# A list schedule that knows TensorE's clock gate

## The chip, the cores and the metric

The kernel runs on one core of a Trainium2 chip. The metric is the device time of one execution in microseconds (us). A core has five engines that run side by side, each through its own queue in order: TensorE (PE, matrix products into PSUM), VectorE (DVE), ScalarE (ACT), GpSimd (POOL) and SyncE (SP, which issues transfers here).

## What is computed

A residual vector quantizer between two depthwise convolutions, on two sequences of 16000 steps with 512 channels in bfloat16:

```python
B, T, D, K = 2, 16000, 512, 3
Nq, C = 4, 8
...
for i in range(K):
    z = z + xp[:, i:i+T, :] * dw_enc[i][None, None, :]
z = _silu(z)
res = z
q = jnp.zeros_like(z)
for s in range(Nq):
    cb = codebooks[s]
    d2 = |res|^2 - 2 res.cb + |cb|^2          # (shortened)
    idx = d2.argmin(-1)
    sel = cb[idx]
    q = q + sel
    res = res - sel
...
for i in range(K):
    y = y + qp[:, i:i+T, :] * dw_dec[i][None, None, :]
```

Each of four stages picks the nearest of eight codewords for each time step and subtracts it from the residual.

## The kernel before

The sequence is cut into 18 tiles (0 to 17): 6 and 8 blocks of 128 steps, fourteen tiles of 16 blocks, then 8 and 6. A tile passes through these kinds of steps, by the names that the scheduler uses:

- "load" and "pad": transposing transfers, and two small copies on GpSimd
- "taps", "exp", "plus1", "recip", "gate": the first convolution and the activation, in two halves (h = 0, 1) of the channels. Taps are multiplications by a scalar and sums on VectorE; exp and recip are table functions on ScalarE, each in its own table; plus1 adds 1 to the exponential and gate multiplies
- "score0", "decide", "win0": small products of the residual with the codebooks, the choice of stages 0 to 2 on VectorE in a long chain of small steps (with transposes and corrections on TensorE), and the one-hot matrix of the choices, which is copied out of PSUM into OHW
- "resid": 24 products that subtract the chosen codewords, each followed by an evacuation
- "score3", "decide3", "win3": the last stage
- "back": the products that give the output, their copies out of PSUM on ScalarE, and the stores

All steps are first collected with their dependences, then put in order by a list scheduler in Python while the program is built, and issued in that order. Nothing of it runs on the chip; it fixes the order of each engine's queue, and which engine takes a step that two engines can do. It works with a cost in microseconds for each step, and among the steps that can start earliest takes the one with the lowest rank:

```python
    def rank(self, s):
        w = self.when[s["k"][0]][self.part(s)]
        return w[0] + s["k"][1] + w[1] * s["k"][2]
...
            full = [d for d in ("ACT", "DVE") if held[d] >= self.quota[d]]
            ...
                dest = "DVE" if load("DVE", t) + self.share[self.part(s)] < load("ACT", t) else "ACT"
...
            if isinstance(s["e"], tuple) and e == "ACT" and t + s["c"]["ACT"] > max(at[s["n"]], clock["DVE"]) + s["c"]["DVE"] + self.slack[self.part(s)]:
                return inf, None
```

SHARE weighs the two engines where a residual product is to be emptied, SLACK where a small step may go to either, and WHEN holds two numbers for each kind of step and each part of the program (tiles 0 to 2, the middle, tiles 15 to 17). A product costs the time of a full clock:

```python
    def mm(n):
        return max(0.06, 0.004 + n / 2380)
```

The residual is the step on which most of the choice bears. With ScalarE as the taker, an identity product first brings the old residual into PSUM and the evacuation is a copy; with VectorE it is an addition (cut):

```python
                    def mms(s=s, u=u, i=i, zg=zg, box=box):
                        on_act = box["dest"] == "ACT"
                        for k0 in range(0, GH, 4):
                            nk = min(4, GH - k0)
                            o = ps(box)[:, k0 * P:(k0 + nk) * P]
                            if on_act:
                                nc.tensor.matmul(o, lhsT=IDENT, rhs=zg[:, k0:k0 + nk, :], start=True, stop=False)
                            nc.tensor.matmul(o, lhsT=CBN[s, u][:, i * P:(i + 1) * P], rhs=W[:, k0:k0 + nk, PADC:PADC + P],
                                             start=not on_act, stop=True)

                    def evac(zg=zg, box=box):
                        v = ps(box)[:, 0:GH * P].rearrange("p (k c) -> p k c", c=P)
                        if box["dest"] == "ACT":
                            nc.scalar.copy(zg, v)
                        else:
                            nc.vector.tensor_tensor(out=zg, in0=zg, in1=v, op=ALU.add)
                    j = add("PE", {"ACT": 2 * mm(GH * P), "DVE": mm(GH * P)}, key, mms, [tok, ("OHW", n % NOH, 0), ("CBN", s, u), "I"], [],
                            take=("A", box), dest="ANY", mm={"ACT": 2 * ((GH + 3) // 4), "DVE": (GH + 3) // 4})
                    add(None, {"ACT": act_psum(GH * P), "DVE": dve(GH * P)}, key, evac, [], [tok], free=box, after=[j])
```

The taps, where either engine may multiply, and the activation:

```python
                dst, src, w = (tb if k else ta)[:, c], X[:, i, k:k + G, :].rearrange("p g c -> p (g c)"), WENC[:, k, i:i + 1]
                either({"ACT": act(R), "DVE": dve(R, 3.84) + 0.06}, key, lambda dst=dst, src=src, w=w: nc.scalar.mul(dst, src, w),
                       lambda dst=dst, src=src, w=w: nc.vector.tensor_scalar(out=dst, in0=src, scalar1=w, scalar2=None, op0=ALU.mult),
                       allx + ["WENC"], [("TB" if k else "TA", c)])
            if k == 1:
                tt(ta, ta, tb, ALU.add, dve(2 * R, 1.92), key, [("TB", 0), ("TB", 1)], [("TA", 0), ("TA", 1)])
        tt(Z, v(ta), v(tb), ALU.add, dve(2 * R, 1.92), key, [(t, c) for t in ("TA", "TB") for c in range(2)], zt)
        add("ACT", act(2 * R), ("exp", n, h), lambda: nc.scalar.activation(v(ex), Z, ACT.Exp, scale=-1.0), zt, [("EX", sl), "ACTTAB"], hold="E")
        either({"ACT": act(2 * R), "DVE": dve(2 * R, 3.84)}, ("plus1", n, h), lambda: nc.scalar.add(ex, ex, 1.0),
               lambda: nc.vector.tensor_scalar(out=ex, in0=ex, scalar1=1.0, scalar2=None, op0=ALU.add), [], [("EX", sl)])
```

PSUM is used as four pairs of banks ("A" takes a pair, "S" one bank):

```python
    PS = [psum.tile([P, 1024], F32, name=f"ps{b}") for b in range(NA)]
```

Of the kernel before, what the change touches and what calls it, by code (L numbers as in the profile page):

```python
# [16 lines left out]
class Plan:  # L17
# [5 lines left out]
    LATENCY = {"PE": 0.2, "ACT": 0.22, "DVE": 0.15, "POOL": 0.25, "SP": 0.1}  # L23
    TABLE = 1.28
    CHUNK, FIRST, FETCH = 128, 33, 4.2

    def __init__(self, pairs, edges, share, slack, quota, when):
        self.steps, self.writer, self.readers = [], {}, {}
        self.pairs, self.edges, self.share, self.slack, self.quota, self.when = pairs, edges, share, slack, quota, when
# [22 lines left out]
    def rank(self, s):  # L52
        w = self.when[s["k"][0]][self.part(s)]
        return w[0] + s["k"][1] + w[1] * s["k"][2]

    def order(self):
        steps = self.steps
        inf = float("inf")
        left = [len(s["deps"]) for s in steps]
        rank = [self.rank(s) for s in steps]  # L60
        users = [[] for _ in steps]
        for s in steps:
            for d in s["deps"]:
                users[d].append(s["n"])
        at = [0.0] * len(steps)
        clock = {e: 0.0 for e in self.LATENCY}
        waiting = {e: [] for e in clock}
        held = {e: 0 for e in clock}
        banks = [0.0] * (2 * self.pairs)
        table = None  # L70
        run, fetched = self.FIRST, 0.0
        self.busy = {e: 0.0 for e in clock}
        out = []

        def cost(s, e):
            return s["c"][e] if isinstance(s["c"], dict) else s["c"]

        def place(kind, t):
            if kind == "A":
                return min((max(banks[j], banks[j + 1], t), 0, j) for j in range(0, 2 * self.pairs, 2))  # L80
            return min((max(banks[j], t), -max(banks[j ^ 1], t), j) for j in range(2 * self.pairs))

        def load(d, t):
            return max(clock[d] - t, 0.0) + held[d] + sum(cost(steps[m], d) for m in waiting[d]
                                                        if at[m] <= t + 1.0 and (d == "DVE" or not isinstance(steps[m]["e"], tuple)))

        def many(s, dest):
            return s["mm"][dest] if isinstance(s["mm"], dict) else s["mm"]

        def late(m, t, c):  # L90

            return max(0.0, fetched - (t + c * (self.CHUNK - run) / m)) if run + m > self.CHUNK else 0.0

        def look(s, e):

            t = max(at[s["n"]], clock[e])
            if s["take"]:
                dest = s["dest"]
                if dest == "ANY":
                    full = [d for d in ("ACT", "DVE") if held[d] >= self.quota[d]]  # L100
                    if len(full) == 2:
                        return inf, None
                    if full:
                        dest = "ACT" if full[0] == "DVE" else "DVE"
                    else:
                        dest = "DVE" if load("DVE", t) + self.share[self.part(s)] < load("ACT", t) else "ACT"
                elif dest and held[dest] >= self.quota[dest]:
                    return inf, None
                kind = s["take"][0]
                t = place(kind[dest] if isinstance(kind, dict) else kind, t)[0]  # L110
                return t + late(many(s, dest), t, cost(s, dest) if s["dest"] == "ANY" else s["c"]), dest
            if isinstance(s["e"], tuple) and e == "ACT" and t + s["c"]["ACT"] > max(at[s["n"]], clock["DVE"]) + s["c"]["DVE"] + self.slack[self.part(s)]:
                return inf, None
            if s["mm"]:
                t += late(s["mm"], t, s["c"])
            return t, None

        def open_(n):
            e = steps[n]["e"]
            for e in e if isinstance(e, tuple) else (e,) if e else ():  # L120
                waiting[e].append(n)

        for s in steps:
            if not left[s["n"]]:
                open_(s["n"])
        while len(out) < len(steps):
            (t, dest), _, n, e = min(((look(steps[n], e), rank[n], n, e) for e, names in waiting.items() for n in names),
                                     key=lambda q: (q[0][0], q[1], q[2], q[3]))
            assert t < inf
            s = steps[n]  # L130
            for w in waiting.values():
                if n in w:
                    w.remove(n)
            c = cost(s, dest if s["take"] and s["dest"] == "ANY" else e)
            if s["take"]:
                kind, box = s["take"]
                kind = kind[dest] if isinstance(kind, dict) else kind
                j = place(kind, t)[2]
                box["banks"] = [j, j + 1] if kind == "A" else [j]
                for j in box["banks"]:  # L140
                    banks[j] = inf
                box["dest"] = dest
                if s["dest"] == "ANY":
                    steps[n + 1]["e"] = dest
                if dest:
                    held[dest] += 1
            elif s["box"] is not None:
                s["box"]["dest"] = e
            if s["hold"] and table != s["hold"]:
                table = s["hold"]  # L150
                c += self.TABLE
            if s["mm"]:
                m = many(s, dest)
                run += m
                if run > self.CHUNK:
                    run -= self.CHUNK
                    fetched = t + c * (m - run) / m + self.FETCH
            s["t"], s["d"], s["on"] = t, c, e
            clock[e] = t + c
            self.busy[e] += c  # L160
            end = t + c + s["tail"]
            if s["free"]:
                if s["free"]["dest"]:
                    held[s["free"]["dest"]] -= 1
                for j in s["free"]["banks"]:
                    banks[j] = end + self.LATENCY[e]
            out.append(s)
            for u in users[n]:
                ue = steps[u]["e"]
                at[u] = max(at[u], t + c + self.AGAIN[e] if ue == e else end + self.LATENCY[e])  # L170
                left[u] -= 1
                if not left[u]:
                    open_(u)
        self.span = max(clock.values())
        return out
# [3 lines left out]
def kernel(  # L179
# [27 lines left out]
    PAIR = 1  # L207
    NX, NE, NZ, NOH, NY = 2, 3, 4, 4, 4
    NA = 4
    SHARE = (14.79, 1.9, -1.12)  # L210
    SLACK = (0.29, -1.21, -1.81)
    QUOTA = {"ACT": 3, "DVE": 4}
    WHEN = {"setup": ((0.456, 0.998), (1.178, 0.655), (0.941, 0.735)), "load": ((-1.978, 0.878), (-1.958, 0.738), (-1.958, 0.878)),
            "pad": ((-1.401, 0.11), (-1.77, 0.139), (-2.325, 0.134)), "taps": ((-0.056, 0.558), (-0.338, 0.569), (0.293, 1.087)),
            "exp": ((1.265, 0.168), (1.206, 0.297), (1.399, 0.12)), "plus1": ((1.063, 0.361), (0.294, 0.173), (0.161, 0.493)),
            "recip": ((0.527, 0.735), (0.419, 0.023), (1.274, 0.525)), "gate": ((-0.093, 0.61), (0.842, 0.495), (1.223, 0.636)),
            "score0": ((-0.15, 0), (1.321, 0.2), (0.126, 0)), "decide": ((1.789, 0.412), (0.54, 0.196), (0.843, 0.939)),
            "win0": ((2.222, 0), (2.206, 0), (3.035, 0.025)), "resid": ((1.585, 0.81), (1.683, 0.7), (1.984, 0.791)),
            "score3": ((2.128, 0.749), (2.581, 0.231), (3.178, 1.482)),
            "decide3": ((1.618, 0.493), (2.772, 0.723), (3.423, 0.605)), "win3": ((2.988, 0.158), (3.009, 1.183), (3.689, 0.224)),  # L220
            "back": ((2.837, 0.37), (3.155, 1.136), (4.316, 0.509))}
    assert B == len(SIZES) and T >= GM * P and GM <= 16

    xf = x.flatten_outer_dims()
# [65 lines left out]

    plan = Plan(NA, (3, len(tiles) - 3), SHARE, SLACK, QUOTA, WHEN)
    add = plan.add
# [506 lines left out]
```

## Time and profile before

| | |
|---|---|
| time, median of 3 | 740.62 us (738.44 to 742.37) |
| profiled execution | 735.13 us, span 733.4 us |
| busy: VectorE, ScalarE, TensorE, GpSimd | 676.7, 665.8, 528.2, 140.0 us |
| mean granted TensorE clock | 0.927 of full |

"Busy" is the time in which an engine has an instruction under way. A row of the costliest groups gives line, engine, operation, what is written and read, the count, then busy time and mean ns of one, then the idle time of the engine just before these instructions and the instruction that ended most of it. The answer on waits gives for each pair of waiter and releaser the sum in us, the number and the longest. The granted clock is a record of its own: it is 1.00 or 0.50 at any time here.

```profile
PEclk9997875897999999998999999999997999999998
```

Each digit is one fortieth of the span, in tenths of the full clock.

### The profile page before, as it was taken

To read this page: it belongs to the slowest core of one execution; us is meant where nothing else is said; L and a number is where in the kernel's file an instruction comes from. 1 tells how busy PE (TensorE), PEld (TensorE's weight loads), DVE (VectorE), ACT (ScalarE), POOL (GpSimd) and SP (SyncE) were. 2 spreads that over 40 slices of the span, in tenths; PEclk is the share of its full clock that TensorE was granted. 3 is DMA by queue.
4 is the path that set the end of the run, shared out by engine and by line. 5 is a ranking of instruction groups with operands and counts; after the bars stand their busy time and mean duration, and the time that the engine had idled before them with its cause. 6 is when DMAs were issued, how large, how long until landed. Compare 5 with 4: busy or idle time off the path is not lost.

```text
span 733.4 us, 23788 instructions
## 1 busy us (share of the span) xinstructions
PE 528.2 (72%) x10374; PEld 269.3 (37%) x10441; DVE 676.7 (92%) x1249; ACT 665.8 (91%) x592; POOL 140.0 (19%) x199
## 2 busy tenths in 40 slices
PE   1055733787868779886797778777867888898994
PEld 0032221443333344443343333433434444444442
DVE  8979999999999999998989999999988999998992
ACT  7868999998999999999899999998987999999755
POOL 2111013030112114332011212212112040111204
PEclk9997875897999999998999999999997999999998
DMA  5554536523361825438073562809343050113306
GB/s 113 95 98 81 129 54 139 91 60 67 109 109 30 146 81 116 110 62 172 11 163 69 87 111 74 156 25 185 59 76 94 10 130 24 61 59 116 117 11 200
DMA packets 148047, 67.78 MB, mean 92 GB/s; under 512 B 139776, under 2 KB 139808, under 8 KB 147944
## 3 DMA queue, kind: packets, MB, share of 16 engines
q1 hardware_dynamic: 137088, 33.06, 26.9%
q0 software_dynamic: 10640, 32.78, 14.8%
q8 instruction: 81, 1.33, 0.8%
q10 hardware_dynamic: 216, 0.43, 0.2%
q14 instruction: 22, 0.18, 0.1%
HBM read 0.43 MB, written 32.77 MB: 45 GB/s over the span
## 4 chain that ended last, share of the span: by engine, by line
DVE 32%; PE 22%; issue 6%; ACT 6%; SPq 1%; DMA 0%; POOL 0%; POOLq 0%; DVEq 0%; ACTq 0%
DVE ZB L668 9%; PE ps L660 7%; PE ps L526 5%; PE ps L659 5%; DVE ZB L333 5%; DVE TB L491 3%; ACT ZB L666 2%; DVE TA L333 2%; ACT YB L725 2%; PE ps L717 2%; DVE OHW L637 2%; DVE TA L491 2%; DVE EX L498 1%; DVE KEY L333 1%; PE ps L631 1%
## 5 line engine op out<-in xcount | busy, mean ns | idle before, releaser
L666 ACT CAST ZB<-ps 128x1024 bf16<-128x1024 f32 (+2 forms) x301 | 259.5, 959 | 34.3 <-PE ps L660 30.9
L660 PE MATMUL ps<-OHW,CBN 128*128 128x512 bf16 (+1 forms) x768 | 271.6, 390 | 17.8 <-DVE ZB L668 7.4
L659 PE MATMUL ps<-ZB,IDENT 128*128 128x512 bf16 (+1 forms) x540 | 212.5, 394 | 28.5 <-ACT ZB L666 10.0
L748 POOL DMA_DIRECT2D out_dram<-YB x130 | 77.6, 601 | 344.8 <-ACT YB L725 341.4
L668 DVE TENSOR_TENSOR ZB<-ZB,ps 128x1024 bf16<-128x1024 bf16 (+2 forms) x131 | 136.7, 1056 | 6.2 <-PE ps L660 5.2
L725 ACT CAST YB<-ps 128x1024 bf16<-128x1024 f32 x126 | 124.7, 1044 | 5.8 <-PE ps L526 2.5
L660 PEld LDWEIGHTS <-CBN 128*128 128x128 bf16 x768 | 75.7, 100 | 140.2 <-issue 70.7
L526 PE MATMUL ps<-ZB 128*32 128x64 bf16 x8064 | 93.1, 202 | 40.2 <-DVE ZB L333 22.4
L496 ACT ACTIVATE EX<-ZB 128x4096 bf16<-128x4096 bf16 (+2 forms) x36 | 115.7, 3215 | 5.1 <-DVE ZB L333 4.9
L508 ACT ACTIVATE EX<-EX 128x4096 bf16<-128x4096 bf16 (+2 forms) x36 | 114.8, 3199 | 0.5 <-DVE EX L498 0.3
L526 PEld LDWEIGHTS <-ZB 128*32 128x32 bf16 x8064 | 80.0, 99 | 88.9 <-issue 66.3
L491 DVE TENSOR_SCALAR TB<-XT,WENC 128x2048 bf16<-128x2048 bf16 (+2 forms) x139 | 93.0, 686 | 0.2
L717 PE MATMUL ps<-WDEC,OHW 128*128 128x512 bf16 x215 | 70.7, 400 | 17.4 <-DVE ZB L668 5.3
L659 PEld LDWEIGHTS <-IDENT 128*128 128x128 bf16 x540 | 54.2, 100 | 67.5 <-issue 13.8
L333 DVE TENSOR_TENSOR ZB<-ZB,EX 128x4096 bf16<-128x4096 bf16 (+2 forms) x36 | 73.5, 2042 | 1.3 <-ACT EX L508 1.1
L333 DVE TENSOR_TENSOR ZB<-TA,TB 128x4096 bf16<-128x4096 bf16 (+2 forms) x36 | 73.4, 2039 | 0.6 <-ACT TB L490 0.4
L333 DVE TENSOR_TENSOR TA<-TA,TB 128x4096 bf16<-128x4096 bf16 (+2 forms) x36 | 73.0, 2027 | 0.4
L469 POOL COPY XT<-XT 128x508 bf16<-128x508 bf16 x18 | 35.5, 1972 | 69.5 <-DVE TB L491 65.5
L491 DVE TENSOR_SCALAR TA<-XT,WENC 128x2048 bf16<-128x2048 bf16 (+2 forms) x70 | 47.7, 692 | 0.6 <-DMA XT<-in_x_dram 0.2
L468 POOL COPY XT<-XT 128x508 bf16<-128x508 bf16 x18 | 24.3, 1353 | 125.1 <-DMA XT<-in_x_dram 125.1
L631 PE MATMUL ps<-IDENT,OHA 128*32 128x128 bf16 x504 | 24.2, 235 | 30.1 <-DVE OHA L333 12.9
L717 PEld LDWEIGHTS <-OHW 128*128 128x128 bf16 x252 | 23.6, 101 | 48.8 <-issue 22.5
(99 smaller groups left out, 433.2 us busy)
## 6 DMA issues: line engine op xcount, KB each, us to landing
out_dram<-YB POOLq DMA_DIRECT2D x33, 448.0 KB, 3.8
out_dram<-YB POOLq DMA_DIRECT2D x28, 512.0 KB, 4.5
XT<-in_x_dram SPq DMA_TRANSPOSE x252, 3.2
out_dram<-YB POOLq DMA_DIRECT2D x30, 60.0 KB, 3.9
out_dram<-YB POOLq DMA_DIRECT2D x31, 2.0 KB, 2.2
out_dram<-YB POOLq DMA_DIRECT2D x2, 224.0 KB, 2.6
YB<-in_dw_dec_dram ACTq DMA_DIRECT2D x1, 384.0 KB, 4.2
out_dram<-YB POOLq DMA_DIRECT2D x1, 384.0 KB
```

The source lines that it names most:

```text
L333: add("DVE", cost, key, lambda: nc.vector.tensor_tensor(out=out, in0=a, in1=b, op=op), reads, writes, **kw)
L491: lambda dst=dst, src=src, w=w: nc.vector.tensor_scalar(out=dst, in0=src, scalar1=w, scalar2=None, op0=ALU.mult),
L496: add("ACT", act(2 * R), ("exp", n, h), lambda: nc.scalar.activation(v(ex), Z, ACT.Exp, scale=-1.0), zt, [("EX", sl), "ACTTAB"], hold="E")
L508: nc.scalar.add_instruction(mybir.InstActivation(name=nc.get_next_instruction_name(), engine=mybir.EngineType.Activation, func=ACT.Reciprocal,
L526: nc.tensor.matmul(o[HB * q:HB * (q + 1), u * ZW:(u + 1) * ZW].rearrange("p (s c) -> p s c", s=2), lhsT=blk, rhs=both, start=False, stop=( ...
L659: nc.tensor.matmul(o, lhsT=IDENT, rhs=zg[:, k0:k0 + nk, :], start=True, stop=False)
L660: nc.tensor.matmul(o, lhsT=CBN[s, u][:, i * P:(i + 1) * P], rhs=W[:, k0:k0 + nk, PADC:PADC + P], start=not on_act, stop=True)
L666: nc.scalar.copy(zg, v)
L668: nc.vector.tensor_tensor(out=zg, in0=zg, in1=v, op=ALU.add)
L717: nc.tensor.matmul(o, lhsT=W[:, k, PADC:PADC + P], rhs=WDEC[u], start=True, stop=not wrap)
L725: add("ACT", act_psum(1024), key, lambda k=k, box=box, Y=Y, k0=k0: nc.scalar.copy(Y[:, 2 * (k - k0):2 * (k - k0) + 2, :].rearrange("p g d ...
L748: nc.gpsimd.dma_start(out=view[p0:p1, lo:hi, :], in_=Y[p0:p1, lo - g0:hi - g0, :])
```

## The change

The scheduler's cost of a product becomes dependent on TensorE's recent use. It counts the work of TensorE in windows of 3.413 us. Where a window held less than half of its length in work, the next one runs at half clock, in which the products of a step take longer by a factor that depends on the kind: 2.0 for the residual and the output, 1.5 for the one-hot windows, 1.4 for the scores, 1.5 for others. The first number of a pair in GATE is the share of the step's time that counts as work. No products are added to keep TensorE busy. The constants SHARE, SLACK and WHEN are new as well. The purpose is an order that suits the times which products really take.

```diff
--- before.py
+++ after.py
@@ -23,6 +23,8 @@
     LATENCY = {"PE": 0.2, "ACT": 0.22, "DVE": 0.15, "POOL": 0.25, "SP": 0.1}
     TABLE = 1.28
     CHUNK, FIRST, FETCH = 128, 33, 4.2
+    SPAN, BUSY = 3.413, 0.5
+    GATE = {"resid": (1.0, 2.0), "back": (1.0, 2.0), "win0": (0.6, 1.5), "win3": (0.6, 1.5), "score0": (0.25, 1.4), "score3": (0.25, 1.4)}
 
     def __init__(self, pairs, edges, share, slack, quota, when):
         self.steps, self.writer, self.readers = [], {}, {}
@@ -53,6 +55,22 @@
         w = self.when[s["k"][0]][self.part(s)]
         return w[0] + s["k"][1] + w[1] * s["k"][2]
 
+    def product(self, t, c, share, half):
+
+        def turn():
+            self.full, self.work, self.turn = self.work >= self.BUSY * self.SPAN, 0.0, self.turn + self.SPAN
+        while self.turn <= t:
+            turn()
+        while c > 1e-9:
+            f = 1.0 if self.full else half
+            d = min(c * f, self.turn - t)
+            c -= d / f
+            t += d
+            self.work += d * share
+            if t >= self.turn - 1e-9:
+                turn()
+        return t
+
     def order(self):
         steps = self.steps
         inf = float("inf")
@@ -69,6 +87,7 @@
         banks = [0.0] * (2 * self.pairs)
         table = None
         run, fetched = self.FIRST, 0.0
+        self.full, self.turn, self.work = False, self.SPAN, 0.0
         self.busy = {e: 0.0 for e in clock}
         out = []
 
@@ -151,6 +170,7 @@
                 c += self.TABLE
             if s["mm"]:
                 m = many(s, dest)
+                c = self.product(t, c, *self.GATE.get(s["k"][0], (0.5, 1.5))) - t
                 run += m
                 if run > self.CHUNK:
                     run -= self.CHUNK
@@ -207,18 +227,17 @@
     PAIR = 1
     NX, NE, NZ, NOH, NY = 2, 3, 4, 4, 4
     NA = 4
-    SHARE = (14.79, 1.9, -1.12)
-    SLACK = (0.29, -1.21, -1.81)
+    SHARE = (16.06, 1.34, -0.93)
+    SLACK = (0.29, -4.95, -2.39)
     QUOTA = {"ACT": 3, "DVE": 4}
-    WHEN = {"setup": ((0.456, 0.998), (1.178, 0.655), (0.941, 0.735)), "load": ((-1.978, 0.878), (-1.958, 0.738), (-1.958, 0.878)),
-            "pad": ((-1.401, 0.11), (-1.77, 0.139), (-2.325, 0.134)), "taps": ((-0.056, 0.558), (-0.338, 0.569), (0.293, 1.087)),
-            "exp": ((1.265, 0.168), (1.206, 0.297), (1.399, 0.12)), "plus1": ((1.063, 0.361), (0.294, 0.173), (0.161, 0.493)),
-            "recip": ((0.527, 0.735), (0.419, 0.023), (1.274, 0.525)), "gate": ((-0.093, 0.61), (0.842, 0.495), (1.223, 0.636)),
-            "score0": ((-0.15, 0), (1.321, 0.2), (0.126, 0)), "decide": ((1.789, 0.412), (0.54, 0.196), (0.843, 0.939)),
-            "win0": ((2.222, 0), (2.206, 0), (3.035, 0.025)), "resid": ((1.585, 0.81), (1.683, 0.7), (1.984, 0.791)),
-            "score3": ((2.128, 0.749), (2.581, 0.231), (3.178, 1.482)),
-            "decide3": ((1.618, 0.493), (2.772, 0.723), (3.423, 0.605)), "win3": ((2.988, 0.158), (3.009, 1.183), (3.689, 0.224)),
-            "back": ((2.837, 0.37), (3.155, 1.136), (4.316, 0.509))}
+    WHEN = {"setup": ((-0.546, 0.828), (0.981, 0.661), (0.636, 0.69)), "load": ((-1.978, 0.906), (-1.958, 0.766), (-1.958, 0.906)),
+            "pad": ((-1.36, 0.11), (-1.729, 0.172), (-2.284, 0.134)), "taps": ((-0.113, 0.582), (-0.347, 0.593), (0.293, 1.111)),
+            "exp": ((1.06, 0.008), (1.152, 0.319), (1.397, 0)), "plus1": ((1.063, 0.15), (0.477, 0), (-0.064, 0.282)),
+            "recip": ((0.527, 0.484), (0.419, 0.417), (1.269, 0.525)), "gate": ((-0.03, 0.594), (0.804, 0.752), (1.299, 0.636)),
+            "score0": ((-0.177, 0.123), (1.294, 0.281), (0.013, 0.081)), "decide": ((1.802, 0.562), (0.602, 0.25), (0.197, 1.08)),
+            "win0": ((2.222, 0), (2.202, 0), (2.375, 0.018)), "resid": ((1.588, 0.66), (1.683, 0.671), (1.853, 0.8)),
+            "score3": ((2.141, 0.68), (2.594, 0.295), (3.143, 1.548)), "decide3": ((2.406, 0.49), (2.769, 0.72), (3.503, 0.602)),
+            "win3": ((2.983, 0.224), (3.004, 1.299), (3.567, 0.29)), "back": ((3.036, 0.427), (3.354, 1.193), (4.185, 0.515))}
     assert B == len(SIZES) and T >= GM * P and GM <= 16
 
     xf = x.flatten_outer_dims()
```

## The prediction, made before the changed kernel was run

> **What bounds the kernel now.** I read the busy shares first, then the idle time of the two busiest engines, then the recorded clock. From the page of the kernel before:
>
> ```profile
> span 733.4 us, 23788 instructions
> PE 528.2 (72%) x10374; PEld 269.3 (37%) x10441; DVE 676.7 (92%) x1249; ACT 665.8 (91%) x592; POOL 140.0 (19%) x199
> DVE 32%; PE 22%; issue 6%; ACT 6%; SPq 1%; DMA 0%; POOL 0%; POOLq 0%; DVEq 0%; ACTq 0%
> L666 ACT CAST ZB<-ps 128x1024 bf16<-128x1024 f32 (+2 forms) x301 | 259.5, 959 | 34.3 <-PE ps L660 30.9
> L668 DVE TENSOR_TENSOR ZB<-ZB,ps 128x1024 bf16<-128x1024 bf16 (+2 forms) x131 | 136.7, 1056 | 6.2 <-PE ps L660 5.2
> ```
>
> VectorE is idle for 733.4 - 676.7 = 56.7 us and ScalarE for 67.6 us. No order of the same instructions on the same engines can gain more than that, and both engines are nearly full at once, so moving work from one to the other gains little. The last two rows are the same job, emptying PSUM into the residual, done by either engine: 301 times on ScalarE and 131 times on VectorE.
>
> Next, the waits of each engine. The largest lines of the two answers:
>
> ```profile
> DVE rr L684 <- PE ps L526: 5.5, 7, 1.7
> DVE rr L560 <- PE ps L526: 5.3, 5, 2.5
> DVE ZB L668 <- PE ps L660: 5.2, 8, 1.7
> ...
> ACT ZB L666 <- PE ps L660: 30.9, 38, 3.6
> ACT EX L496 <- DVE ZB L333: 4.9, 5, 1.7
> ```
>
> Adding all lines of VectorE's answer that name PE gives about 33 us, and of ScalarE's about 43 us. So waits for TensorE are the largest part of the idle time, many (38 for one line) and short. That is what a better order can reach.
>
> Third, how much of it lies where TensorE ran at half clock. Dividing the span at the first recorded half-clock stretch (63.48 us) and at the last instruction of the compute engines (about 729), and then asking for the half-clock stretches alone, gives these rows (columns: length, then busy time of PE, weight loads, DVE, ACT, POOL, granted clock, DMA share, GB/s). The last one is the sum over all half-clock stretches, in which one of 6.28 us after the end of the compute is contained:
>
> ```profile
> 0.00:63.48 63.48, 19.14 (x410) 11.47 (x410) 54.42 (x155) 48.91 (x87) 8.83 (x38) 1.00 0.53 101
> 63.48:729.08 665.60, 509.06 (x9964) 257.85 (x10031) 622.33 (x1095) 616.86 (x506) 130.11 (x159) 0.92 0.42 92
> ...
> sum 108.68, PE 66.98 PEld 32.81 DVE 94.24 ACT 87.35 POOL 21.57; mean PE 4.19 PEld 2.05 DVE 5.89 ACT 5.46 POOL 1.35
> ```
>
> In the middle part VectorE is idle 665.60 - 622.33 = 43.3 us and ScalarE 48.7 us. Half clock covers 108.68 - 6.28 = 102.4 us of it, with VectorE idle 8.2 us and ScalarE 15.1 us. The other 563.2 us have 35.1 us (6.2%) and 33.7 us (6.0%). If the half-clock stretches had only those shares, they would have 6.4 and 6.1 us. So the idle time that half clock adds is about **2 us on VectorE and 9 us on ScalarE**. This is the room of what the change is named for, and it is small. The reading of 1.00 before 63.48 us means only that no clock event is recorded there.
>
> [...] its half-clock stretches last 3.41, 6.83, 10.24 or 17.07 us. [...] the first one starts 63.48 us after the first instruction, which is 18.6 windows, while the new model lets a window begin at zero. [...] At N = 512 the trace has starts 0.42 to 0.43 us apart from 302.79 to 305.35 us, and 0.21 to 0.22 us at 302.19 and 302.40. That is the factor of 2.0 that the table of the change gives to "resid" and "back". [...]
>
> **The change part by part.** The chip gets no new kind of instruction. What is new is the order on all engines, and who takes the work that either engine can do. I compared the instructions of the two programs by engine.
>
> (a) Work that moves to VectorE, at the means of the trace by shape. Wide residual adds, 97 to 101: 4 x 1.214 = +4.9 us. Narrow ones, 20 to 19: -0.55. One more addition of 1 to the exponential, 27 to 28: +1.23. Small copies OT (+3 and -1, at 0.22): +0.45. One OHW copy of three blocks: +0.36. One CBN scaling: +0.34. Taps: -0.41 - 0.48 + 0.42 = -0.48. Sum: **VectorE +6.2 us**, to 682.9.
>
> (b) The same for ScalarE. Wide evacuations 239 to 235: 4 x 1.042 = -4.2. Narrow ones +0.6. The one addition of 1 that it did: -3.6. OT about -0.55, OHW -0.5, CBN -0.7. Taps: +0.94 + 1.13 - 0.93 = +1.1. Sum: **ScalarE -7.8 us**, to 658.0. The two engines together have 1.6 us less. Both orders alternate exponential and reciprocal in the same pairs, so there are still 36 table loads.
>
> (c) TensorE: each evacuation by ScalarE needs the identity product that brings the old residual into PSUM, so there are eight fewer of 512 columns and one more of 384. At a step of 0.215 us that is -1.6 us on an engine that is busy 72%: nothing by itself.
>
> (d) The order. Counting runs of equal work in the two programs, little changes in kind. On TensorE the output products stand in 90 runs of at most 3, where there were 86 of at most 5, and residual products in 124 runs against 122. On ScalarE 14 exponentials of 36 stand between two residual evacuations, against 12. In the ramp, the residual of tile 0 starts before tile 1's scores on TensorE, and the first scores are read two taps later on VectorE. The last two tiles keep nearly the same order, with one evacuation of tile 16 and one of tile 17 given to ScalarE. Adjacent VectorE steps of which the second needs the first are 84 before and 80 after. Neither the tail nor the dependent chains change much.
>
> **What it comes to.** VectorE leads in the chain (32% against ScalarE's 6%), so I charge (a) in full: +6. Against it stands what the new order saves of VectorE's 43 us of idle time in the middle. Half clock itself gives at most 2 us there directly; ScalarE's 9 us count only as far as a late evacuation delays the next product and so VectorE. I take half of the two together, 5.5 us. The constants were also fitted anew, over all parts of the span. I estimate that this takes about a fifth off the 33 us which VectorE waits for TensorE, some 6.5 us. That fifth is a judgement, not a count. Sum: +6 - 5.5 - 6.5 = -6 us, from 740.6 to about **735 us**.
>
> **The rivals.** First, a full VectorE: the work moved in (a) is paid and the waits stay as they are. Then 740.6 + 6.2 = 747 us. For it speaks that VectorE is already the fullest engine and that its idle time is in many short waits, which come back elsewhere when one is removed. Against it, ScalarE gets 7.8 us of room, and much of what VectorE waits for depends on ScalarE's evacuations. Second, a chaotic replay: in-order queues of five engines and four pairs of PSUM banks let one misplaced instruction hold up the rest, and the model's clock is off in phase. The new order then holds waits of a new kind, such as ScalarE's longest for line 666 above, 3.6 us; ten of 2 us each would give 755 to 760 us. The scale of the constants speaks for it (the slack of the middle tiles goes from -1.21 to -4.95); that the order keeps its form speaks against. Third, a large gain: the better model removes two thirds of VectorE's 33 us of waits. Less the 6 us of (a) this would be about 724 us. For it: PE waits are the largest class on both engines. Against: only some 11 us can be tied to half clock.
>
> **Range and chances.** The centre is 735. The range goes from 722, a little beyond the large gain, to 750, a little beyond the full VectorE. A move of 2% is 14.8 us: faster would mean below 725.8, a third of VectorE's middle idle time plus the 6 us moved to it, which I give 0.15. Slower would mean above 755.4, the chaotic replay alone, 0.08. The rest, 0.77, is within 2%. Repeats of the kernel before lie between 738.4 and 742.4, so a change of 6 us should show.
>
> **What would show it.** Step (a) is right if VectorE's busy time is 681 to 685 us and ScalarE's 656 to 660. The clock step is right if the half-clock stretches hold much less than 15 us of ScalarE's idle time, while their length stays near 100 us; if the length falls a lot, the order has made TensorE less quiet, which I do not expect. The step on the waits is right if VectorE's lines that name PE fall from 33 to 20 to 25 us. The prediction is wrong if VectorE's idle time stays near 57 us (full VectorE), or falls below 40 us (large gain), or if single waits of over 3 us stand in the middle (chaotic replay).

## The result and the profile after

The changed kernel takes 731.63 us (median of 4, 731.18 to 733.01) against 741.5 us for the kernel before: a ratio of 0.987, with a 95% interval of 0.983 to 0.991. When it was run again beside the experiments, the ratio was 0.985 (0.980 to 0.989). The prediction was 735 us.

The page of the changed kernel. Its lines 678, 679, 685, 687 and 744 are lines 659, 660, 666, 668 and 725 of the kernel before, 19 further down:

```profile
span 731.2 us, 23783 instructions
PE 539.4 (74%) x10370; PEld 272.3 (37%) x10434; DVE 681.8 (93%) x1256; ACT 660.7 (90%) x585; POOL 138.0 (19%) x199
DVE 16%; PE 10%; ACT 3%; issue 3%; POOL 0%; POOLq 0%; DVEq 0%; ACTq 0%
L685 ACT CAST ZB<-ps 128x1024 bf16<-128x1024 f32 (+2 forms) x298 | 257.3, 938 | 39.9 <-PE ps L679 37.9
L687 DVE TENSOR_TENSOR ZB<-ZB,ps 128x1024 bf16<-128x1024 bf16 (+2 forms) x134 | 140.4, 1064 | 6.2 <-PE ps L679 3.9
```

VectorE works 5 us more than in the first profile of before and is idle 49.4 us instead of 56.7; ScalarE works 5 us less. The chain that ended last can be followed back over only a third of the span here (16 + 10 + 3 + 3%), against two thirds before, so its shares are not compared. The longest waits of the two engines, with the sum, the number and the longest:

```profile
DVE rr L579 <- PE ps L545: 6.6, 8, 2.7
DVE ZB L687 <- PE ps L679: 3.9, 8, 1.6
DVE rr L703 <- PE ps L545: 3.7, 4, 1.7
...
ACT ZB L685 <- PE ps L679: 37.9, 63, 4.2
ACT YB L744 <- PE ps L736: 4.3, 5, 2.0
```

All of VectorE's waits on TensorE come to 25.8 us (33.5 before), all of ScalarE's to 46.4 us (43.4). Of the two engines, only VectorE waits less.

The middle part of the span, from the first recorded half-clock stretch to the last one after the compute, and then the sum over the half-clock stretches of this part:

```profile
60.58:726.18 665.60, 519.03 (x9960) 260.42 (x10024) 629.64 (x1107) 613.15 (x499) 128.57 (x159) 0.91 0.42 92
...
sum 126.29, PE 90.28 PEld 42.33 DVE 120.65 ACT 108.15 POOL 23.91; mean PE 4.75 PEld 2.23 DVE 6.35 ACT 5.69 POOL 1.26
```

TensorE is **not** slow for less time: 126 us at half clock, where the first profile of before had 102 us. But VectorE is idle for only 126.29 - 120.65 = 5.6 us of it (8.2 us of 102 before).

The profiles of before and after differ by 2 us, the medians by 10. So a second profile of the kernel before is needed; it comes with the experiments.

### The profile page after: what moved, and what is told of

Same layout as the page of the kernel before. It is cut to its first block, busy times and chain, and to the rows that moved or that the text cites. A ratio compares the mean times of both kernels' runs of the same rounds, so it can differ in the third digit from the quotient of the medians.

```text
span 731.2 us, 23783 instructions
## 1 busy us (share of the span) xinstructions
PE 539.4 (74%) x10370; PEld 272.3 (37%) x10434; DVE 681.8 (93%) x1256; ACT 660.7 (90%) x585; POOL 138.0 (19%) x199
## 3 DMA queue, kind: packets, MB, share of 16 engines
q0 software_dynamic: 10640, 32.78, 14.6%
## 5 line engine op out<-in xcount | busy, mean ns | idle before, releaser
L679 PE MATMUL ps<-OHW,CBN 128*128 128x512 bf16 (+1 forms) x768 | 275.8, 396 | 26.8 <-DVE ZB L687 16.3
L678 PE MATMUL ps<-ZB,IDENT 128*128 128x512 bf16 (+1 forms) x533 | 215.1, 404 | 26.8 <-ACT ZB L685 12.1
L687 DVE TENSOR_TENSOR ZB<-ZB,ps 128x1024 bf16<-128x1024 bf16 (+2 forms) x134 | 140.4, 1064 | 6.2 <-PE ps L679 3.9
L545 PE MATMUL ps<-ZB 128*32 128x64 bf16 x8064 | 95.1, 202 | 33.4 <-DVE ZB L352 19.6
L678 PEld LDWEIGHTS <-IDENT 128*128 128x128 bf16 x533 | 54.9, 103 | 69.5 <-issue 19.6
L736 PE MATMUL ps<-WDEC,OHW 128*128 128x512 bf16 x206 | 69.5, 403 | 11.5 <-DVE ZB L687 6.6
L487 POOL COPY XT<-XT 128x508 bf16<-128x508 bf16 x18 | 25.4, 1409 | 127.5 <-DMA XT<-in_x_dram 108.2
L488 POOL COPY XT<-XT 128x508 bf16<-128x508 bf16 x18 | 32.2, 1788 | 69.1 <-DVE TB L510 65.3
L517 DVE TENSOR_SCALAR EX<-EX 128x4096 bf16<-128x4096 bf16 (+2 forms) x36 | 40.6, 1129 | 0.4 <-ACT EX L515 0.4
```

Of the source, the lines that this page charges most:

```text
L545: nc.tensor.matmul(o[HB * q:HB * (q + 1), u * ZW:(u + 1) * ZW].rearrange("p (s c) -> p s c", s=2), lhsT=blk, rhs=both, start=False, stop=( ...
L736: nc.tensor.matmul(o, lhsT=W[:, k, PADC:PADC + P], rhs=WDEC[u], start=True, stop=not wrap)
```

## The experiments

**Theory.** The gain comes from an order that was fitted against products which slow down after a quiet window: it bears half clock without making VectorE wait. **Rivals:** the new constants alone; another division of the work between VectorE and ScalarE; more searching, whatever the model; room for slower products in general; an order that keeps TensorE awake; or one lucky order among many.

Does the chip slow down as the scheduler assumes? The 14 profiles of this case can answer that. In the first profile of before the half-clock stretches of the middle last 3.41 us or 2, 3 or 5 times that, in the second up to 40.95 us, 12 times that. So I cut the recorded clock into windows of 3.41 us. All 256 windows in which TensorE was busy for less than 40% were followed by one at half clock, and 1609 of the 1617 in which it was busy for more than 80% by one at full clock. From 40 to 50% it was half clock 109 times of 147, from 50 to 80% 120 times of 789. So the scheduler's limit of one half comes near what these traces show, but is not sharp in them.

**The kernel before again**, unchanged.

> The kernel before, unchanged, for a second profile and for the spread of its times: 738 to 746 us, ratio 0.997 to 1.003. If its profile of 733.4 us was a short draw among its runs, the idle time of VectorE is now above 57 us, 60 to 66 us, with the same busy time.

It took 741.27 us (20 runs), ratio 0.998 (0.995 to 1.000). Its profile shows the middle part, two of the half-clock stretches, and the sum over all of them:

```profile
64.08:736.51 672.43, 513.47 (x9964) 261.12 (x10031) 623.40 (x1093) 616.96 (x506) 128.26 (x159) 0.91 0.43 91
...
514.64:518.06 3.42, 3.18 (x70) 1.72 (x70) 2.06 (x5) 1.13 (x2) 0.00 (x0) 0.50 1.74 273
562.43:572.67 10.24, 7.38 (x169) 4.24 (x169) 7.62 (x20) 6.83 (x3) 0.98 (x1) 0.50 0.11 37
...
sum 126.31, PE 80.51 PEld 42.95 DVE 112.04 ACT 106.72 POOL 20.95; mean PE 6.19 PEld 3.30 DVE 8.62 ACT 8.21 POOL 1.61
```

This is the same half-clock time as in the changed kernel (126.3 us), so the two can be compared. VectorE is idle for 126.31 - 112.04 = 14.3 us of it, 11.3%, against 34.8 us or 6.4% in the rest of the middle (546.1 us). By the reckoning of the prediction half clock adds 14.3 - 0.064 x 126.3 = 6.2 us, not 2. In the changed kernel it adds nothing: 5.6 us or 4.5%, against 5.6% in the rest. The profile on which the prediction rested was a run with little half clock. The expected 60 to 66 us of idle time were met: 740.9 - 678.3 = 62.6 us.

What such a stretch does is seen in this profile's timeline of 562 to 572 us (start, duration, engine and line; in brackets the idle time before and what ended it):

```profile
564.07 0.59 PE L520 MATMUL ps<-MSK,IDENT 128*128 128x512 bf16 x1 [3.54 <-DVE PR L685]
564.58 1.90 PE L526 MATMUL ps<-ZB 128*32 128x64 bf16 x128
566.28 1.05 PE L631 MATMUL ps<-IDENT,OHA 128*32 128x128 bf16 x24
567.38 0.42 DVE L560 TENSOR_REDUCE rr<-ps 128x8 f32<-128x256 f32 x1 [1.71 <-PE ps L631]
571.61 1.01 ACT L666 CAST ZB<-ps 128x1024 bf16<-128x1024 f32 x1 [3.36 <-PE ps L660]
```

TensorE stood for 3.54 us and then ran at half clock: its 128 score products take 1.90 us, where 128 at full clock took 1.22 us in the first profile (at 313.90 us). VectorE waits 1.71 us before it reads the scores; the trace puts this wait down to the 24 one-hot products (line 631) that come right behind them. ScalarE waits 3.36 us for the residual products that follow. How much of these waits is due to half clock, and how much to the 3.54 us in which TensorE stood, the trace does not say. The first profile of before has the same place at 555 us.

**The changed kernel again**, unchanged.

> The changed kernel, unchanged, for the spread of its times against the half-clock time of each run. Over 58 runs of the kernel before, a run's time grows by 0.21 us for each us at half clock (correlation 0.75), with 122 us at half clock on average. If the new order bears half clock better, not less of it: 730 to 734 us, about 120 us at half clock, and a slope of 0.05 to 0.1. If the new order gains by something else: the same slope of about 0.2 at a lower level. Ratio 0.983 to 0.99.

It took 732.18 us (6 runs). Each run has its granted clock, and as the first profiles of both kernels record only 1.00 and 0.50, twice the missing share times the span is taken as its half-clock time: 2 x 0.090 x 731.2 = 131.6 us for the first profile of the changed kernel, where the recorded half-clock stretches sum to 133.4 us (in the profiles of the two kernels 4 to 5 us of this lie at the end, when no product runs any more). Over 133 runs of the kernel before (one of 1309 us is left out) that is 93 to 148 us, and the time rises with it by **0.22 us per us** (95% interval 0.19 to 0.25, correlation 0.75): runs below 110 us take 739.2 us in the mean, those above 130 us 745.2 us. The 10 runs of the changed kernel, at 104 to 132 us, show no rise: a slope of -0.03 (-0.22 to 0.06). At the common 120 us the two are 11 us apart. But the two runs below 110 us take 732.4 us in the mean, 7 us less than the kernel before there, so only the part of the gain above that grows with half-clock time. Half clock and time could both follow from a third thing, and ten runs are few, so the slope alone proves no cause.

The profile of this run has less half clock, and is best set beside the first profile of before, which had 102.4 us:

```profile
63.76:725.95 662.19, 522.53 (x10024) 257.66 (x10024) 625.22 (x1101) 610.58 (x499) 124.07 (x159) 0.92 0.42 92
...
sum 109.25, PE 77.46 PEld 35.53 DVE 102.72 ACT 91.75 POOL 19.72; mean PE 4.56 PEld 2.09 DVE 6.04 ACT 5.40 POOL 1.16
```

VectorE's idle time in the middle falls from 43.3 to 37.0 us. Of these 6.3 us only 1.6 lie in the half-clock stretches (8.2 to 6.5) and 4.7 outside. In the pair with 126 us it was 8.6 us inside and 4.4 outside. So the theory covers two thirds of VectorE's saving in one pair and a quarter in the other; why VectorE waits less outside these stretches was not shown.

**The gate out of the scheduler, new constants kept.**

```diff
-                c = self.product(t, c, *self.GATE.get(s["k"][0], (0.5, 1.5))) - t
```

> The new constants, with the scheduler's clock gate taken out (a product always costs the time of the full clock). If the gate model itself places the work, its removal loses most of the gain of 1.3%: ratio to the kernel before 0.995 to 1.01. If the newly fitted constants alone carry the gain, the ratio stays at 0.985 to 0.99. A third reading, that constants and model were fitted to each other, expects it above 1.0.

744.1 us, ratio 1.003 (1.001 to 1.006). The new constants alone carry nothing. Its profile happens to have the half-clock time of the changed kernel (126.29 us):

```profile
sum 126.31, PE 84.21 PEld 41.32 DVE 115.20 ACT 104.23 POOL 21.57; mean PE 5.26 PEld 2.58 DVE 7.20 ACT 6.51 POOL 1.35
```

VectorE is idle for 11.1 us of it, where it was 5.6 with the gate, and works 3.1 us more over the span (684.9 us). These two make 8.6 of the 10.6 us by which this span is longer (741.8 against 731.2 us). With one profile on each side, this is the clearest sign that the gate in the scheduler changes what half clock costs.

**The gate in the scheduler, old constants kept.**

```diff
-    SHARE = (16.06, 1.34, -0.93)
+    SHARE = (14.79, 1.9, -1.12)
     (SLACK and WHEN as in the kernel before, too)
```

> The clock gate in the scheduler, with the constants of the kernel before. If the gate model by itself is worth something: 0.985 to 0.995. If the gain is that of the fitted constants: 1.00 to 1.01. If constants fit only the model that they were fitted with: 1.01 to 1.03.

749.98 us, ratio 1.010 (1.006 to 1.013). The gate alone carries nothing either: the gain is in the pair, as the third reading of both runs has it (here at the lower edge of its range). This order, too, leaves VectorE idle for only 4.4 us of 122.9 us at half clock, but ScalarE for 34.5 us, and it gives VectorE 693.0 us of work. Little idle time of VectorE at half clock is thus not enough by itself.

**The scheduler's windows shifted by half a window.**

```diff
-        self.full, self.turn, self.work = False, self.SPAN, 0.0
+        self.full, self.turn, self.work = False, 0.5 * self.SPAN, 0.0
```

> The changed kernel with the scheduler's windows shifted by half a window (1.7 us). If the phase of the model means nothing on the chip, what is left is the effect of another order of the same kind: within 0.5% of the changed kernel, 0.983 to 0.992. If orders are so sensitive that only the fitted one is good, 0.995 to 1.01.

760.94 us, ratio 1.024 (1.020 to 1.028), far above both ranges. The shift is not a shift on the chip; it is another order, for which the constants were not fitted. So it does not tell whether the phase matters on the chip. It tells that orders of the same kind differ by 4%, three times the gain, so that a single order can be better or worse by luck. Its waits:

```profile
DVE rr L703 <- PE ps L545: 12.2, 6, 3.7
DVE rr L579 <- PE ps L545: 7.0, 6, 2.8
...
ACT ZB L685 <- PE ps L679: 53.0, 67, 4.0
ACT EX L515 <- DVE ZB L352: 19.5, 8, 7.2
```

**Fitting in either scheduler.** If fitting decides, the question is whether the gate in the scheduler makes a fitted order better. I searched for constants with the shortest schedule, by the scheduler's own reckoning, crosswise: with the gate, from the constants of the kernel before.

```diff
-    SHARE = (16.06, 1.34, -0.93)
+    (SHARE, SLACK and WHEN found by the search, scheduler as in the changed kernel)
```

> The scheduler with the gate, and constants found by my own search for the shortest schedule in it, started from the constants of the kernel before. The scheduler's own length is 696.5 us, against 694.0 us in the changed kernel and 719.1 us with the constants of the kernel before. If the gain comes from fitting an order against products that slow down after quiet windows, this other order has most of it: 731 to 738 us, ratio 0.983 to 0.993. If the order of the changed kernel is one lucky draw: 742 to 755 us, ratio 0.998 to 1.015.

737.82 us, ratio 0.996 (0.993 to 0.999). Faster than the kernel before, but between the two ranges: about a third of the gain comes back, so a lucky draw is not ruled out for the rest. And without the gate, from the constants of the changed kernel:

```diff
-    SHARE = (14.79, 1.9, -1.12)
+    (SHARE, SLACK and WHEN found by the search, scheduler as in the kernel before)
```

> The scheduler without the gate, and constants found by the same search, started from the constants of the changed kernel. Its own length is 688.7 us, against 687.2 us in the kernel before and 697.3 us with the constants unfitted. If fitting without the gate has no more to give: 740 to 750 us, ratio 0.996 to 1.01. If more searching from the new constants is what helped, whatever the model: 728 to 736 us, ratio 0.98 to 0.99.

747.23 us, ratio 1.007 (1.004 to 1.010), as the theory expects; this one further search without the gate does not help. In its half-clock stretches VectorE is idle 16.9 us of 146.8, or 11.5% as in the second profile of before; with the gate (the run above) 7.8 us of 109.3, or 7.2%, not far from the 8.0% in the first profile of before at 102 us.

**Products slower throughout, without windows**, and fitted by the same search.

```diff
     def product(self, t, c, share, half):
-        (the windows)
+        return t + 1.12 * c
     (SHARE, SLACK and WHEN found by the search)
```

> The scheduler without windows: every product costs 1.12 times its full-clock time, which is about what the gate adds on average (528 us of products in the changed kernel's own schedule against 473 without the gate), and constants found by the same search in this scheduler, started from those of the changed kernel (its own length 700.2 us). If room for slower products is all that the gate model gives: 731 to 738 us, ratio 0.983 to 0.993. If the window logic matters, that is, which products are slow: 741 to 752 us, ratio 0.998 to 1.012.

741.63 us, ratio 1.000 (0.998 to 1.003). Room for slow products in general brought nothing. This fits the reading that it matters which products are slow, but does not prove it: the fit with windows above is 4 us faster, with one order on each side, from different starting constants, where orders differ by up to 4%. The sum over the half-clock stretches:

```profile
sum 112.63, PE 70.20 PEld 36.36 DVE 92.81 ACT 89.42 POOL 18.79; mean PE 4.13 PEld 2.14 DVE 5.46 ACT 5.26 POOL 1.10
```

VectorE is idle for 19.8 us of them, 17.6%, against 24.1 us or 4.3% in the other 563.2 us of the middle. Of all the profiles here this has the least idle share outside the half-clock stretches and the largest inside.

**The division of the work.** The order stays as in the changed kernel, but twelve wide evacuations change engine.

```diff
+        for s in steps:
+            n = s["k"][1]
+            if s["k"][0] == "resid" and s["take"] and s["take"][1]["dest"] == "DVE" and 3 <= n < 15 and n not in moved:
+                moved.add(n)
+                s["take"][1]["dest"] = "ACT"
```

> The order of the changed kernel, with one wide residual evacuation in each of tiles 3 to 14 given from VectorE to ScalarE: VectorE 12 x 1.21 = 14.6 us less work, ScalarE 12 x 1.04 = 12.5 us more, TensorE 24 more identity products (5 us). If VectorE alone sets the time, as the prediction charged it, about 719 to 723 us, ratio 0.97 to 0.975. If the two engines share the bound evenly, 731 to 736 us, ratio 0.987 to 0.993. If ScalarE is the tighter one, 738 to 745 us, ratio about 1.0.

757.79 us, ratio 1.019 (1.015 to 1.023). None of the three readings holds: VectorE has 12 us less work and the kernel is 26 us slower than the changed one. Page and largest wait:

```profile
PE 554.7 (73%) x10458; PEld 275.2 (36%) x10458; DVE 669.5 (88%) x1244; ACT 671.3 (89%) x597; POOL 120.1 (16%) x199
...
DVE ZB L687 <- PE ps L679: 21.1, 15, 4.8
```

VectorE's wait for the products of its own evacuations grows from 3.9 to 21.1 us. That the identity products and copies put in its way hold them up is the likely reason, but was not tried apart. The other way round ("ACT" to "DVE" in the same lines):

> The counterpart of the run with twelve evacuations given to ScalarE, which was 3.3% slower than the changed kernel: here one wide evacuation in each of tiles 3 to 14 goes from ScalarE to VectorE, with the order as it is. VectorE has 14.6 us more work, ScalarE 12.5 us less, TensorE 24 products less. If VectorE alone set the time: 731.6 + 14.6 = 746 us, ratio 1.003. If what matters is that each step stands where its engine and its bank are free when it comes, any twelve moves cost about the same as the other twelve: 750 to 760 us, ratio 1.01 to 1.025, with idle time grown on both engines.

744.66 us, ratio 1.003 (1.000 to 1.005), as if VectorE alone set the time: twelve additions cost 12.6 us over the changed kernel (732.1 us over its ten runs). Busy times of its profile:

```profile
PE 527.9 (71%) x10346; PEld 266.6 (36%) x10410; DVE 692.9 (94%) x1268; ACT 650.1 (88%) x573; POOL 127.1 (17%) x199
```

So work added to VectorE is paid nearly in full (12.6 of 14.6 us), and work taken from it in a fixed order is not repaid. Neither run makes the new division (four wide evacuations more on VectorE) a source of the gain; a division fitted together with its order was not tried apart.

**TensorE kept at work** by products that change nothing: the mask product, which opens a score group, is repeated ahead of itself.

```diff
+                for _ in range(6 if st["n"] < 5 else 0):
+                    nc.tensor.matmul(o, lhsT=IDENT, rhs=MSK[:, 0:nb, :], start=True, stop=True)
                 nc.tensor.matmul(o, lhsT=IDENT, rhs=MSK[:, 0:nb, :], start=True, stop=False)
```

> The kernel before, with six extra products of the mask ahead of each of the 16 score groups of tiles 0 to 4, in the same order otherwise; their result is overwritten by the product that follows, so they only keep TensorE at work: 96 products, 21 us at full clock. If half clock is what the old order loses by: half-clock time falls by some 30 us from 122, and the time by 0.21 of that, to 736 us, ratio 0.99. If the products only stand in the way of the scores: 748 to 760 us, ratio 1.007 to 1.02.

765.6 us, ratio 1.026 (1.020 to 1.032), above both ranges, with 108 us at half clock in the median of its runs. And in the changed kernel:

> The same 96 extra products in the changed kernel. If its order already bears half clock, there is nothing to gain: 730 to 736 us, ratio 0.983 to 0.991, with half-clock time some 30 us shorter. If half clock still costs it as much as the kernel before: 724 to 727 us. If the products stand in the way: above 738 us.

749.07 us, ratio 1.007 (1.004 to 1.010), 103 us at half clock, and over 17 runs the time rises again with half clock, by 0.31 us per us. Both are slower by about the length of the 96 products (21 us at full clock, estimated from the 0.215 us between starts of 512 columns in the first profile of before), though half clock is shorter by some 10 to 18 us (30 were expected). VectorE's longest waits in the first of the two (the profile is of the fastest of its six runs, 755.62 us; its lines are 2 further down than in the kernel before):

```profile
DVE rr L686 <- PE ps L528: 17.0, 13, 3.5
DVE rr L562 <- PE ps L528: 11.7, 5, 4.4
```

These are the waits for the scores (6.4 and 5.6 us in the second profile of the kernel before): the products stand in line ahead of them. The test says that waking TensorE this way does not pay. It does not say what half clock alone would cost.

## Why the prediction was right

**Step (a), VectorE +6.2 us to 682.9:** measured 681.8 and, in the second profile, 679.4 us. **Step (b), ScalarE -7.8 us to 658.0:** measured 660.7 and 660.0 us. Both have the right sign. But the kernel before had 676.7 and 678.3 us on VectorE, and 665.8 and 666.4 us on ScalarE, so between the means of two profiles the change is +3.1 us, half of what was put down for (a), and -5.8 us for (b). That work added to VectorE is to be charged nearly in full is borne out by the twelve additions, each of which cost 12.6 / 12 = 1.05 us of 1.21.

**The clock step** was the term that was mis-sized. "At most 2 us there directly" came from one profile with 102 us at half clock. A profile with 126 us gives 6.2 us, and the changed kernel, also at 126 us, has -1.5 us by the same reckoning: 7.7 us on VectorE alone, where 5.5 us were put down for both engines. Between the two profiles with 102 and 109 us it is only 1.8 - 0.5 = 1.3 us. So the term is no fixed amount, and one profile cannot size it; the half-clock time itself, expected near 100 us, was 126 and 109 us. The sign given for ScalarE was wrong: its idle time at half clock was to fall well below 15 us, and it is 18.1 us of 126.3 us (19.6 in the comparable profile of before). ScalarE goes on waiting; VectorE is idle there no more than elsewhere (4.5% against 5.6%).

**The waits:** VectorE's waits on TensorE were to fall from 33 to between 20 and 25 us. They are 25.8 and 26.7 us, just above, from 33.5 and 39.6: a fall by a fifth to a third. The fifth that was a judgement has about the right size. But it and the clock step overlap: a wait for TensorE at half clock counts in both. VectorE's idle time in the middle falls by 13.1 us (49.0 to 36.0) in the pair with 126 us, two thirds of it at half clock, and by 6.3 us in the other pair, a quarter of it at half clock.

**The sum:** -6 us predicted, -10 us measured, inside the range. That the two overlapping terms, one of them read from a run with little half clock, came to nearly the right sum is partly luck. Of the rivals, the full VectorE is refuted by the fall of its idle time from 56.7 and 62.6 to 49.4 and 50.9 us, and the large gain did not come. The sign set for the chaotic replay, single waits of over 3 us, was met by ScalarE's longest wait for TensorE (4.2 and 3.5 us), but the kernel before had 3.6 and 3.4 us, so the sign could not tell the two apart. The in-order queues from which that rival argues are seen in the first profile of before: all 1249 instructions of VectorE and all 592 of ScalarE run in the order of issue. The times show no chaotic replay in the changed kernel; the shifted window shows how near it is.

One reading needs a correction: the trace of before does record full clock from 49.84 to 63.50 us. Only before that is nothing recorded; 128 score products at 47.15 us took 1.90 us there, as long as at half clock, so the half-clock sums leave out the start of the program.

What stays open: two orders fitted with the gate gave 0.985 and 0.996. Both beat the three fitted without windows (1 for the kernel before, 1.007 and 1.000), but the two are further from each other than the poorer one is from the kernel before. That gate and constants must go together is shown for this one order; that fitting with the gate gives a gain of this size in general is not. The poorer one's runs still get longer with half clock (0.18 us per us). By the scheduler's own reckoning it is 2.5 us longer than the changed kernel; whether that is the reason was not shown.

## What to carry to other kernels

Where a program's order is found by a model, look for what its costs leave out and the trace shows: here adding the one state that makes products up to twice as long (in the first profile of before, starts of 512 columns lie 0.42 to 0.43 us apart at half clock and 0.21 to 0.22 at full), and fitting again, brought 1.3% in one fit and 0.4% in another, while either half of this alone brought nothing. Read how much a throttle costs from several runs with different throttled time, not from one profile. And a fitted order is brittle: change one rule in it and fit again before judging the rule.

## What had not been expected

- The same program spends between 93 and 148 us at half clock from run to run, and for the kernel before the time follows at 0.22 us per us.
- Orders of one kernel with nearly the same work (VectorE busy 670 to 693 us) lay between 731 and 761 us.
- Products added to keep the clock up cost 17 and 22 us, about what they last, although TensorE is busy for only 72 to 74% of the span in the profiles of the two kernels without them (528.2 and 539.4 us).
